# Transposes of attention output and second norm through DMA, other query blocks and merged logits in an adaLN attention and FFN layer

## The chip, the cores and the metric

The program runs on one core of a Trainium2 chip. The metric is the device time of one execution in microseconds. Three runs of the kernel before gave 216.83, 216.92 and 216.99 us, median 216.92 us.

## What is computed

One transformer layer on 2048 tokens of width D = 448 in bf16. The vector `c` gives six modulation vectors; a layer norm, scaled and shifted by two of them, feeds an attention with 16 heads of 28; each query sees 8 keys, at its own position and 2, 4, ... 14 before it. Its output goes through `wo`, is gated and added to `x`. A second modulated norm feeds a gated silu FFN of width 1792.

```python
mod = (silu(c) @ w_mod).reshape(1, 6, 1, -1)          # sa, ca, ga, sb, cb, gb
h = layernorm(x) * (1 + ca) + sa
q, k, v = split_heads(h @ wqkv)                       # 16 heads of 28
idx = pos[:, None] - arange(8)[None, :] * 2           # masked where < 0
attn = softmax(einsum('bhsd,bhswd->bhsw', q, k[idx]) * 28 ** -0.5)
x = x + ga * (einsum('bhsw,bhswd->bhsd', attn, v[idx]) @ wo)
h = layernorm(x) * (1 + cb) + sb
x = x + gb * (silu(h @ w1) @ w2)
```

## The kernel before

The keys of a token have its parity, so the tokens are split by parity (`par`) into two sequences of 1024. A token tile is 128 tokens of one parity; a chunk `k` is 256 tokens of each parity, four tiles, and there are four chunks. Within a parity the 1024 queries are cut into nine blocks `b` (`BQ = 114`, the last of 112), each with 128 keys that begin 14 tokens of the original sequence before it; `HALO` columns of zeros in `qk` stand for keys before the first token.

For each chunk, `norm1` (the class `Norm`, lines 404 to 450) takes statistics on DVE (`stat`, L412 and L413), the inverse deviation on POOL (`rstd`, L416 and L417), normalises on DVE (`norm`, L421), transposes a tile on PE (`tr`, L427 for three pieces of 128 columns, L429 twice for the last 64, which is kept on both halves of the partitions) and scales and shifts on ACT or DVE out of PSUM (`mod`, L436 or L438) into `h1`. `project` multiplies by `wqkv`: q and k into `qk` (matmuls L516, casts L520), v for each block (L539, casts L529).

For each block and parity, `logits` computes 16 heads in two calls of eight small matmuls (L569; contraction over the 28 rows of a head, keys on the partitions of the result), with an Exp on ACT behind each call (L577), and `mask` multiplies by a band of ones on DVE (L599). `values` multiplies by v (L626), normalises on DVE (L631, L633) into a tile `o`, transposes it on PE (`tr`, L639 and L641) into `ps_ot` and copies that on ACT or DVE (`tc_`, L644) into `oT`. `out_proj` (L663) contracts over the 448 rows of `oT` and adds the result to `x_all` on DVE (L666).

`ffn1` is a second `Norm` with L427 to L438 into `h2`, and seven pairs of 128x512 tiles of `ps_h` (L687 for three full pieces of the contraction, L689 for the last 64 rows) with a Silu behind each (L693). `ffn2` (L711) sums 14 matmuls of 448 columns for each token tile, adds on DVE (L716) and stores through SP (L717).

A contraction over 448 is three pieces of 128 rows and a rest of 64. For the rest, two independent matmuls use the two halves of the array:

```python
for kk in range(KT):                                  # L538, and in the same way L661
    for par in range(2):
        w = wqkv[:, kk, 2 * D:3 * D] if kk < 3 else wqkv3[half(par), 1, :]
        T.matmul(ps[:, par, 0:D], lhsT=h[rows_of(kk, par), kk, par, b0:b0 + 128], rhs=w, ...)
```

All of it is recorded as operations of a `Plan` with engine, estimated time, dependencies and buffers; `emit` then issues them in the order of the table of numbers `ORDER` (L43), in which a letter picks ACT or DVE where either can do it. Every engine executes its own instructions strictly in that order. PSUM has three tiles of two banks (`big`) and two of one (`one`). The attention blocks and FFN chunks alternate as in `SEQ` (L40): blocks 0 to 4, chunk 0, blocks 5 and 6, chunk 1, blocks 7 and 8, chunks 2 and 3, because Exp and Silu need different tables on ACT. At the start, matmuls on a tile `junk` (L349) keep PE at work. The loads stand first on SP's queue. At the end a count of finite normalisers decides on a second, safe computation, which does not run here.

## Time and profile before

| | before |
|---|---|
| median of three runs | 216.92 us |
| the profiled execution, its own time | 217.79 us |
| its span in the trace | 216.1 us |
| PE busy, matmuls | 201.6 us (93%), 1652 matmuls |
| DVE, ACT, POOL busy | 111.8, 107.3, 21.6 us |
| mean granted TensorE clock | 0.987 of full speed |
| packets of the main DMA queue, share of 16 engines | 15.5% |

Busy times of one engine do not overlap, those of different engines do. The trace names a group by its source line and by what it writes and reads (`ps_h<-h,w`), with the buffer numbers left out. PE is pipelined, so the time that one matmul takes from the stream is the distance between starts, and not its duration; the chain of waits gives that distance for each run of matmuls.

### The profile page before, as it was taken

Reading aid. Unit: us, or ns where it says so; the run is one execution under the profiler, and the core shown is the slowest. Engines: PE = TensorE matmul, PEld = TensorE weight load, DVE = VectorE, ACT = ScalarE, POOL = GpSimd, SP = SyncE. Lnnn points to the kernel's source line nnn. Section 1 sums busy time; section 2 is a strip of 40 time slices with the busy share of each in tenths; the row PEclk is TensorE's granted clock in tenths of the full one; section 3 lists DMA queues with packets and bytes.
Section 4 is the critical chain, followed back from the end, with each engine's and each line's share of the span. In section 5 each row is a group of like instructions: output and inputs, shape, how many; then the busy total and the mean of one; then the engine's idle time right before and its main releaser. Section 6 shows DMA issues by size and latency. Waiting matters only on the chain.

```text
span 216.1 us, 3926 instructions
## 1 busy us (share of the span) xinstructions
PE 201.6 (93%) x1652; PEld 96.3 (45%) x1652; DVE 111.8 (52%) x246; ACT 107.3 (50%) x127; POOL 21.6 (10%) x65
## 2 busy tenths in 40 slices
PE   5799999859999999999999999999998999999990
PEld 1273364434455555434534444555543443445540
DVE  3608934798679886255361620898518441102220
ACT  2006538784487487744755966860453243550000
POOL 6501530000000330010100000111000110000000
PEclk9999999988999999999999999999999999999998
DMA  6999920000000000000000000000100000001111
GB/s 220 321 397 324 353 90 3 0 0 3 0 3 2 3 0 3 0 0 0 3 2 21 24 0 3 0 24 21 42 3 21 0 18 6 21 2 44 46 46 29
DMA packets 7936, 11.33 MB, mean 52 GB/s; under 512 B 552, under 2 KB 6696, under 8 KB 7912
## 3 DMA queue, kind: packets, MB, share of 16 engines
q1 hardware_dynamic: 7904, 11.01, 15.5%
q8 instruction: 15, 0.25, 0.5%
q14 instruction: 9, 0.07, 0.1%
q10 hardware_dynamic: 8, 0.00, 0.0%
HBM read 9.18 MB, written 1.84 MB: 51 GB/s over the span
## 4 chain that ended last, share of the span: by engine, by line
PE 88%; DVE 4%; ACT 2%; DMA 2%; issue 1%; ACTq 0%
PE ps_y L711 20%; PE ps_h L687 18%; PE ps_qk L516 13%; PE ps_v L539 6%; PE ps_wo L663 5%; PE ps_t L427 4%; PE ps_o L626 4%; PE ps_h L689 4%; PE ps_l L569 3%; PE ps_w L349 3%; PE ps_m L378 3%; PE ps_t L429 3%; DMA c<-in_c_dram 2%; PE ps_ot L639 1%; PE ps_ot L641 1%; DVE w L739 1%
## 5 line engine op out<-in xcount | busy, mean ns | idle before, releaser
L711 PE MATMUL ps_y<-w,both 128*128 128x448 bf16 x224 | 45.8, 353 | 0.0
L687 PE MATMUL ps_h<-h,w 128*128 128x512 bf16 x168 | 40.8, 380 | 0.0
L693 ACT ACTIVATE both<-ps_h 128x1024 bf16<-128x1024 f32 x28 | 28.6, 1024 | 23.5 <-PE ps_h L689 14.3
L577 ACT ACTIVATE p<-ps_l 128x912 bf16<-128x912 f32 (+1 forms) x36 | 31.3, 933 | 8.7 <-PE ps_l L569 8.5
L711 PEld LDWEIGHTS <-both 128*128 128x128 bf16 x224 | 20.5, 98 | 19.8 <-issue 1.2
L516 PE MATMUL ps_qk<-h,wp 128*128 128x512 bf16 (+1 forms) x128 | 28.5, 392 | 0.0
L716 DVE TENSOR_TENSOR ot<-ps_y,x_all 128x448 bf16<-128x448 f32 x16 | 9.9, 622 | 32.2 <-PE ps_y L711 32.2
L687 PEld LDWEIGHTS <-w 128*128 128x128 bf16 x168 | 14.7, 97 | 18.9 <-issue 4.0
L520 ACT CAST qk<-ps_qk 128x1024 bf16<-128x1024 f32 x14 | 14.1, 1013 | 16.5 <-PE ps_qk L516 16.5
L416 POOL TENSOR_TENSOR rs<-mv,epsb 128x2 f32<-128x2 f32 (+1 forms) x18 | 6.1, 337 | 151.2 <-DVE mv L413 151.2
L412 DVE BATCH_NORM_STATS2 st<-x_all 128x6 f32<-128x448 bf16 x32 | 19.5, 609 | 2.6 <-DMA x_all<-in_A_x_dram 2.4
L599 DVE TENSOR_TENSOR p<-p,maskb 128x1824 bf16<-128x1824 bf16 (+1 forms) x18 | 19.5, 1094 | 2.4 <-ACT p L577 2.3
L436 ACT ACTIVATE h<-ps_t,modc 128x512 bf16<-128x512 bf16 x14 | 10.1, 774 | 20.7 <-DVE h L438 18.4
L438 DVE TENSOR_SCALAR h<-ps_t,modc 128x512 bf16<-128x512 bf16 x18 | 8.9, 539 | 13.9 <-ACT h L436 8.3
L516 PEld LDWEIGHTS <-wp 128*128 128x128 bf16 (+1 forms) x128 | 9.3, 98 | 15.0 <-issue 7.0
L666 DVE TENSOR_TENSOR x_all<-ps_wo,x_all 128x448 bf16<-128x448 f32 x16 | 9.5, 615 | 9.7 <-PE ps_wo L663 9.7
L539 PE MATMUL ps_v<-wqkv,h 128*128 128x448 bf16 (+1 forms) x72 | 14.3, 355 | 0.0
L569 PE MATMUL ps_l<-qk 28*128 28x114 bf16 (+1 forms) x288 | 11.7, 210 | 2.3 <-ACT p L577 1.2
L421 DVE TENSOR_SCALAR xn<-x_all,mv,rs 128x448 bf16<-128x448 bf16 x32 | 11.6, 385 | 3.9 <-POOL rs L417 3.9
L663 PE MATMUL ps_wo<-wo,oT 128*128 128x448 bf16 (+1 forms) x64 | 12.8, 354 | 0.3 <-ACT p L577 0.3
L417 POOL TENSOR_TENSOR rs<-rs,negh 128x2 f32<-128x2 f32 (+1 forms) x18 | 12.1, 670 | 1.4
L631 DVE RECIPROCAL rc<-ps_o 114x16 f32<-114x16 f32 (+1 forms) x18 | 4.5, 252 | 14.4 <-PE ps_o L626 14.2
(78 smaller groups left out, 185.2 us busy)
## 6 DMA issues: line engine op xcount, KB each, us to landing
x_all<-in_A_x_dram SPq DMA_DIRECT2D x4, 448.0 KB, 7.6
out_dram<-ot SPq DMA_DIRECT2D x16, 112.0 KB, 1.7
w<-in_B_w_dram SPq DMA_DIRECT2D x1, 1568.0 KB
both<-in_w_mod_dram SPq DMA_DIRECT2D x1, 1344.0 KB
w<-in_B_w_dram SPq DMA_DIRECT2D x1, 1344.0 KB, 14.0
wqkv<-in_A_wqkv_dram SPq DMA_DIRECT2D x1, 1008.0 KB, 7.9
both<-in_w_mod_dram SPq DMA_DIRECT2D x1, 672.0 KB, 5.4
wo<-in_A_wo_dram SPq DMA_DIRECT2D x1, 336.0 KB, 10.1
```

The source lines that it names most:

```text
L412: V.bn_stats(out=st[:], in_=x_all[:, us[j], :])
L417: G.tensor_tensor(out=rs[:, j:j + n], in0=rs[:, j:j + n], in1=negh[:, 0:n], op=ALU.pow)
L516: T.matmul(ps[:, j, :], lhsT=w.rearrange("p h d -> p (h d)"), rhs=h[rows_of(kk, j), kk, :, 128:128 + CP], start=start, stop=stop)
L520: return [(either(act_ns(1024), dve_ns(1024)), lambda o, ps: copy_on(o)(out=qk[:, :, g, :, s0:s0 + CP], in_=ps[:].rearrange("p j (t s) -> ...
L539: T.matmul(ps[:, par, 0:D], lhsT=h[rows_of(kk, par), kk, par, b0:b0 + 128], rhs=w, start=(kk == 0), stop=(kk == KT - 1))
L569: T.matmul(ps[:, j, g * nq:(g + 1) * nq], lhsT=key, rhs=q, start=True, stop=True)
L577: S.activation(out=out_, in_=ps[:, :, 0:4 * nq].rearrange("p j (g q) -> p j g q", q=nq), func=ACTF.Exp, scale=SCALE)
L599: V.tensor_tensor(out=p, in0=p, in1=maskb[:, 1 if b == 0 else 0, 0:nq].unsqueeze(1).to_broadcast([128, H, nq]), op=ALU.mult)
L663: T.matmul(ps[:, par, 0:D], lhsT=oT[rows_of(kk, par), kk, par, s0:s0 + 128], rhs=wo[rows_of(kk, par), kk, :], start=(kk == 0), stop=(kk == ...
L687: T.matmul(ps[:, j, :], lhsT=w1[:, kk, c0:c0 + 128], rhs=h[:, kk, :], start=start, stop=stop)
L693: return [(("act", act_ns(1024)), lambda o, ps: S.activation(out=hid[:, k % 2, :, i, :], in_=ps[:], func=ACTF.Silu), after + f2_read.get(k ...
L711: T.matmul(box["ps"][:, 0:D], lhsT=hid[:, k % 2, f % 2, f // 2, 128 * j:128 * j + 128], rhs=w2[:, f // 2 + 7 * (f % 2), :], start=(f == 0) ...
```

## The change

The transposes of the attention output `o` and of the second norm leave PE and become DMA transposes on SP's queue (L669, L465), from SBUF straight into `oT` and `h2`; the second norm is scaled and shifted afterwards, in place in `h2` (L472, L474). The first norm stays on PE, with four transposes of full width in place of five. Block 0 has 128 queries and the other eight have 112, so keys begin at `112 * b` and no halo is needed. A block's two logits calls become one with 16 matmuls whose head rows take turns over the four row groups (L601). Rests of a contraction are either filled up to 128 rows with zeros (the modulation vectors L382, the gates L398) or put so that two rests are neighbours (v and `wo`: even ones end with the rest, odd ones begin with it). For odd positions `o` is written 64 columns further right, and `wo` is held twice, the second time shifted by 64 rows; both are gated. The load of the first `x` chunk is split in two and 392 KB more of `wo` are loaded. `junk` matmuls at the start: 11, then three behind each of the four transposed tiles. Buffers: `v` 8 (9), `xn` two of four tiles each (six single ones), `o` two per parity (three). `Plan` gets SP as an engine; `ORDER` is new.

```diff
+def q_of(b):
+    return 0 if b == 0 else 16 + 112 * b
 def nq_of(b):
-    return min(BQ, SP_ - BQ * b)
+    return 128 if b == 0 else 112
...
-    ld_o = [load(336, wo[:, 0:3, :], rows3(A_wo)), load(56, wo[half(0), 3, :], A_wo[384:D, :]), load(56, wo[half(1), 3, :], A_wo[384:D, :])]
+    ld_o = [load(336, wo[:, 0, 0:3, :], rows3(A_wo)), load(56, wo[half(0), 0, 3, :], A_wo[384:D, :]),
+            load(336, wo[:, 1, 1:4, :], A_wo[K3:D, :].rearrange("(k p) n -> p k n", p=128)), load(56, wo[half(1), 1, 0, :], A_wo[0:K3, :])]
...
             for j in range(KT):
-                    for h in range(1 + (j == 3)):
-                        out_ = ps[0][rows_of(j, h), i, j:j + 1]
-                        c0 = v * D + 128 * j
-                        for k in range(KT):
-                            T.matmul(out_, lhsT=wmod[rows_of(k), k, c0:c0 + (K3 if j == 3 else 128)], rhs=scT[rows_of(k), k:k + 1], ...)
+                    c0 = v * D + 128 * j
+                    for k in range(KT):
+                        T.matmul(ps[0][:, i, j:j + 1], lhsT=wmod[:, k, c0:c0 + 128], rhs=scT[:, k:k + 1], ...)
...
-                for k in range(3):
-                    T.transpose(box["ps"][:, k, 128 * j:128 * j + 128], box[j][:, 128 * k:128 * k + 128], ident[:])
-                for h in range(2):
-                    T.transpose(box["ps"][half(h), 3, 128 * j:128 * j + 128], box[j][:, 384:D], ident[:])
+                for k in range(KT):
+                    T.transpose(box["ps"][:, k, at], box["x"][:, j, 128 * k:128 * k + 128], ident[:])
+                if junk_n:
+                    warm_up(junk_n)
...
+        def on_dma(self, h, waits):
+            def tr(o, j):
+                nc.sync.dma_start_transpose(out=h[:, j:j + 2, :, :].rearrange("p j k t -> p (j k) t"), in_=self.box["x"][:, j:j + 2, :].rearrange("p j n -> p (j n)"))
+            def mod(o, k):
+                for to, from_ in ([(half(1), half(0)), (half(0), half(0))] if k == 3 else [(slice(0, 128),) * 2]):
+                    out_, in_ = h[to, :, k, :], h[from_, :, k, :]
...
             def vmm(o, b=b, held=held):
-                b0 = 128 + BQ * b - 14 - CP * k
-                for kk in range(KT):
+                b0 = 128 + 112 * b - CP * k
+                ks = (0, 1, 2, 3) if b % 2 == 0 else (3, 0, 1, 2)
+                for kk in ks:
...
-        for t in range(2):
-            def mm(o, t=t, held=held):
-                ps = held[0] = bigt("ps_l")
-                for g in range(4):
-                    for j in range(2):
+        def mm(o):
+            for t in range(2):
+                held[t] = bigt("ps_l")
+            for g in range(4):
+                for t in range(2):
+                    for j in range(2):
...
         def tr(o):
-            box["t"] = one.tile([128, KT, 128], BF16, name="ps_ot", tag="one")
-            for kk in range(3):
-                T.transpose(box["t"][:, kk, 0:nq], box["o"][0:nq, 128 * kk:128 * kk + 128], ident[0:nq, 0:nq])
-            for h in range(2):
-                T.transpose(box["t"][half(h), 3, 0:nq], box["o"][0:nq, 384:D], ident[0:nq, 0:nq])
-        def tc_(o):
-            copy_on(o)(out=oT[:, :, par, BQ * b:BQ * b + nq], in_=box["t"][:, :, 0:nq])
+            nc.sync.dma_start_transpose(out=oT[:, :, par, q_of(b):q_of(b) + nq], in_=box["o"][0:nq, :])
...
-            for kk in range(KT):
+            qs = (0, 1, 2, 3) if i == 0 else (3, 0, 1, 2)
+            for q in qs:
                 for par in range(2):
-                    T.matmul(ps[:, par, 0:D], lhsT=oT[rows_of(kk, par), kk, par, s0:s0 + 128], rhs=wo[rows_of(kk, par), kk, :], ...)
+                    kk = q if par == 0 else (q + 1) % KT
+                    rows = slice(0, 128) if q < 3 else half(par)
+                    T.matmul(ps[:, par, 0:D], lhsT=oT[rows, kk, par, s0:s0 + 128], rhs=wo[rows, par, kk, :], ...)
```

What the new order does is seen at three places. The first is SP's queue behind the loads (`o`, `xn`: sources; `ot`: output tiles). Before:

```order
L301 DMA w_79<-in_B_w_dram 128x3x1792
L301 DMA w_80<-in_B_w_dram 64x896 x2
L301 DMA w_81<-in_B_w_dram 128x14x448
L717 DMA out_dram<-ot_111 128x448
L717 DMA out_dram<-ot_112 128x448
```

Now, from the second transposes of the first chunk on:

```order
L465 DMA_TRANSPOSE h_0_87<-xn_81 128x8x128
L669 DMA_TRANSPOSE oT<-o_0_102 128x4x112
L669 DMA_TRANSPOSE oT<-o_0_104 128x4x112
L465 DMA_TRANSPOSE h_1_88<-xn_82 128x8x128 x2
L717 DMA out_dram<-ot_106 128x448
L717 DMA out_dram<-ot_107 128x448
L669 DMA_TRANSPOSE oT<-o_1_103 128x4x112
L717 DMA out_dram<-ot_108 128x448
L669 DMA_TRANSPOSE oT<-o_1_105 128x4x112
```

Where only stores stood behind the loads, 18 transposes of `o` and 8 of `xn` (two token tiles each) stand among the 16 stores; one that comes behind a store waits until the store's tile is there.

The second place is DVE at the second norm of chunk 0, just before the first `ps_h`. Before:

```order
L421 TENSOR_SCALAR xn_83<-x_all,mv,rs 128x448
L421 TENSOR_SCALAR xn_85<-x_all,mv,rs 128x448
L631 RECIPROCAL rc<-ps_o 114x16
L633 TENSOR_TENSOR o_110<-ps_o,rc 114x448
L438 TENSOR_SCALAR h_0_92<-ps_t,modc 128x512 x2
L644 COPY oT<-ps_ot 128x4x114
L599 TENSOR_TENSOR p_107<-p_107,maskb 128x1824
```

Now:

```order
L426 TENSOR_SCALAR xn_81<-x_all,mv,rs 128x448
L664 RECIPROCAL rc<-ps_o 112x16
L665 TENSOR_TENSOR o_0_102<-ps_o,rc 112x448
L633 TENSOR_TENSOR p_101<-p_101,maskb 128x1792
L474 TENSOR_SCALAR h_0_87<-h_0_87,modc 128x4x128 x2
L693 TENSOR_TENSOR x_all<-ps_wo,x_all 128x448 x2
L551 CAST qk<-ps_qk 128x2x2x256
```

The last `xn` tile (first row) now goes to SP's queue; the scaling of `h` follows three instructions later, and the copies into `oT` are gone. Casts of q and k (last row), which for chunk 3 stood behind the first `ps_h`, stand ahead of or around it.

The third place is ACT in the first FFN chunk, around the last Silu before the Exps of block 5. Before:

```order
L693 ACT_TABLE_LOAD
L693 ACTIVATE both<-ps_h 128x2x512 x2
L529 CAST v_95<-ps_v 128x16x28
L693 ACTIVATE both<-ps_h 128x2x512 x5
L577 ACT_TABLE_LOAD
L577 ACTIVATE p_104<-ps_l 128x912 x2
```

Now:

```order
L721 ACT_TABLE_LOAD
L721 ACTIVATE both<-ps_h 128x2x512 x3
L560 CAST v_90<-ps_v 128x16x28
L721 ACTIVATE both<-ps_h 128x2x512 x3
L472 ACTIVATE h_1_88<-h_1_88,modc 128x4x128
L721 ACTIVATE both<-ps_h 128x2x512
L609 ACT_TABLE_LOAD
L609 ACTIVATE p_97<-ps_l 128x896 x2
```

A part of chunk 1's second norm, which needs its transpose, stands ahead of the seventh Silu and of the Exps of block 5.

## Rows read from the trace of the kernel before

**Rows 1.** The page: its head, and busy time by engine.
```profile
span 216.1 us, 3926 instructions
PE 201.6 (93%) x1652; PEld 96.3 (45%) x1652; DVE 111.8 (52%) x246; ACT 107.3 (50%) x127; POOL 21.6 (10%) x65
```

**Rows 2.** Windows: stretch, its length, busy us of PE, PEld, DVE, ACT, POOL, clock, DMA.
```profile
20.06:86.28 66.22, 62.40 (x670) 31.78 (x669) 50.11 (x106) 44.17 (x58) 8.76 (x16) 0.97 0.14 47
86.28:210.44 124.16, 123.35 (x905) 56.67 (x901) 52.02 (x108) 58.97 (x64) 6.16 (x12) 1.00 0.05 15
```

**Rows 3.** Chain of waits, the start: start us, us, engine, tile, line.
```profile
7.17 3.53 PE ps_w L349 x8
10.70 3.15 PE ps_m L378 x40
...
16.57 3.49 PE ps_w L349 x9
```

**Rows 4.** Chain of waits, operations on PE that the change touches.
```profile
28.21 2.81 PE ps_m L378 x40
...
76.45 0.27 PE ps_t L427 x3
...
76.90 0.27 PE ps_t L427 x3
...
110.30 3.35 PE ps_qk L516 x16
...
113.64 0.39 PE ps_o L626 x16
...
136.28 0.26 PE ps_ot L639 x3
...
136.71 0.30 PE ps_l L569 x8
...
138.99 0.33 PE ps_l L569 x16
```

**Rows 5.** Chain of waits, from the last output projection to the end.
```profile
169.32 1.43 PE ps_wo L663 x8
...
176.78 0.27 PE ps_t L427 x3
...
188.09 2.59 PE ps_h L687 x12
...
192.62 17.80 PE ps_y L711 x94
210.44 0.62 DVE ot L716
```

**Rows 6.** Timeline of DVE and of ACT, first scaling of the first norm.
```profile
16.62 1.00 DVE L438 TENSOR_SCALAR h<-ps_t,modc 128x512 bf16<-128x512 bf16 x2 [2.31 <-PE ps_t L429]
17.71 1.45 ACT L436 ACTIVATE h<-ps_t,modc 128x512 bf16<-128x512 bf16 x2 [10.34 <-DVE h L438]
```

**Rows 7.** Groups by line and shape, DVE: busy us, mean ns.
```profile
L599 DVE TENSOR_TENSOR p<-p,maskb 128x1824 bf16<-128x1824 bf16 x16 | 17.4, 1096 | 2.4 <-ACT p L577 2.3
L412 DVE BATCH_NORM_STATS2 st<-x_all 128x6 f32<-128x448 bf16 x32 | 19.5, 609 | 2.6 <-DMA x_all<-in_A_x_dram 2.4
L644 DVE COPY oT<-ps_ot 128x456 bf16<-128x456 bf16 x9 | 3.5, 389 | 2.8 <-PE ps_ot L641 2.8
L520 DVE CAST qk<-ps_qk 128x1024 bf16<-128x1024 f32 x2 | 2.5, 1225 | 1.8 <-PE ps_qk L516 1.8
L738 DVE TENSOR_TENSOR wo<-wo,gbc 128x1792 bf16<-128x1792 bf16 x1 | 1.1, 1082 | 0.0
L633 DVE TENSOR_TENSOR o<-ps_o,rc 114x448 bf16<-114x448 f32 x16 | 10.0, 624 | 0.6
```

**Rows 8.** DMA: time from issue to landing of the stores (L717), and of the `x` loads.
```profile
DMA to landing us min/median/max: 1.7/1.7/2.5
...
x_all<-in_A_x_dram SPq DMA_DIRECT2D x4, 448.0 KB, 7.6
```

More of the change, by code (lines that the diff above doesn't have):

```diff
@@ L259, in rows3 @@
         return ap[0:384, :].rearrange("(k p) n -> p k n", p=128)
-    S.preload_act_table(ACTF.Silu)
-    V.memset(junk[:], 0.0)
-    V.memset(c4[:], 0.0)
+    V.memset(junk, 0.0)
+    V.memset(wmod[half(0), 3, :], 0.0)
     G.memset(ident[:], 0.0)
@@ L281, in layer @@
     P = Plan()
[L282 removed]
+    for r, n in (("big", 3), ("one", 2), ("v", NV), ("p", NP), ("xn", NX), ("o0", 2), ("o1", 2), ("out", len(outb))):
         P.resource(r, n)
@@ L344, in layer, with warm_up @@
     warm = []
-    def warm_up(o):
+    def warm_up(n):
         if not warm:
             warm.append(bigt("ps_w"))
-        T.matmul(warm[0][:, 0, :], lhsT=junk[:, 0:128], rhs=junk[:], start=True, stop=True)
-    w_first = w_last = P.op(("pe", WARM_AT), warm_up if not safe else none, take=("big",), mac=213.0)
-    for i in range(WARM):
-        w_last = P.op(("pe", 213.0), warm_up if not safe else none, [w_last], mac=213.0)
-    P.op(("none", 0.0), none, [w_last], give=((w_first, "big"),))
+        for _ in range(n):
+            T.matmul(warm[0][:, 0, :], lhsT=junk[:, 0:128], rhs=junk, start=True, stop=True)
+    w_first = P.op(("pe", 600.0), none, take=("big",))
+    w_last = P.op(("pe", 213.0 * WARM), lambda o: warm_up(WARM), [w_first], mac=213.0 * WARM)
     sc_op = P.op(("act", 200.0), lambda o: S.activation(out=sc4[:], in_=c4[:], func=ACTF.Silu), ld_c, table="s")
@@ L382, in ev @@
             V.tensor_scalar(out=modc[:, dst0 + 1, :], in0=ps[0][:, 1, :], scalar1=1.0, scalar2=None, op0=ALU.add)
-        a = P.op(("pe", 1050.0), mm, [sct] + loads, take=("one",))
-        return P.op(("dve", 130.0), ev, [a], give=((a, "one"),))
+        a = P.op(("pe", 900.0), mm, [sct] + loads, take=("one",))
+        return P.op(("dve", 150.0), ev, [a], give=((a, "one"),))
     wmod_read = []
@@ L393, in mm @@
             for k in range(KT):
-                T.matmul(ps[0][:, 0:D], lhsT=screp[rows_of(k), k, :], rhs=wmod[rows_of(k), k, v * D:(v + 1) * D], start=(k == 0), stop=(k == KT - 1))
-        a = P.op(("pe", 870.0), mm, [rep] + loads, take=("one",), mac=653.0)
+                T.matmul(ps[0][:, 0:D], lhsT=screp[:, k, :], rhs=wmod[:, k, v * D:(v + 1) * D], start=(k == 0), stop=(k == KT - 1))
+        a = P.op(("pe", 760.0), mm, [rep] + loads, take=("one",), mac=653.0)
         wmod_read.append(a)
@@ L500, in norm1 @@
         after = [x for kk in (k - 2,) if kk >= 0 for x in qk_mm[kk] + v_mm[kk] + [halo[kk + 1]]]
-        n = Norm([4 * k + 2 * i + par for par in range(2) for i in range(2)], {u: ld_x[k] for u in range(4 * k, 4 * k + 4)},
-                 lambda kt: h[:, kt, :, 128:128 + CP], lambda ps: ps.rearrange("p (t s) -> p t s", t=2), 0, after=after, waits=[mod1], behind=h1_tr.get(k - 1, []), n=2 if k else 1)
+        n = Norm([4 * k + j for j in range(4)], {4 * k + j: ld_x[k][j // 2] for j in range(4)}, after=after + h1_tr.get(k - 1, []), n=2 if k else 1)
+        n.on_pe((0, 2, 1, 3), lambda rows, kt: h[rows, kt, :, 128:128 + CP], lambda ps: ps.rearrange("p (t s) -> p t s", t=2), [mod1], 0 if k else JUNK)
+        if k == 0:
+            P.op(("none", 0.0), none, n.trs, give=((w_first, "big"),))
         h1_tr[k] = n.trs
@@ L649, in values @@
             P.need(v_op[bb], [nr])
-        tt = P.op(("pe", 290.0), tr, [nr], take=("one",), give=((a, "o"),), mac=190.0)
-        trs[b, par] = P.op(either(430.0, 305.0), tc_, [tt], give=((tt, "one"),))
+        trs[b, par] = P.op(("sp", 1250.0), tr, [nr] + ld_2, give=((a, f"o{par}"),))
     def out_proj(k, i):
@@ L680, in ffn1 @@
         h = h2[k % 2]
-        nrm = Norm(us_of(k), x1_done, lambda kt: h[:, kt, :], lambda ps: ps, 1, after=f1_read.get(k - 2, []), waits=[mod2])
+        nrm = Norm(us_of(k), x1_done, after=f1_read.get(k - 2, []))
+        nrm.on_dma(h, [mod2])
         def mm(i):
@@ L726, in ffn2 @@
             ad = P.op(("dve", 540.0), add, [prev], take=("out",), give=((first, "one"),))
-            P.op(("none", 0.0), none, [P.op(("none", 2200.0), none, [ad])], give=((ad, "out"),))
+            P.op(("none", 0.0), none, [P.op(("none", 2200.0), none, [P.op(("sp", 550.0), store, [ad])])], give=((ad, "out"),))
     for k in range(NC):
```

234 lines of the change are left out of this document (122 added, 112 removed), and 37 rows, old and new, of the table ORDER.

## Prediction, made before the changed kernel ran

> **What bounds the kernel now.** I read first the busy times of the page: PE has 201.6 of 216.1 us [rows 1], twice what DVE or ACT have. Then the windows, cut where the chain of waits shows the first value matmul (20.06), the first `ps_h` of the FFN (86.28) and the last matmul (210.44). In the first stage, attention with all of chunk 0's second norm, PE is busy 62.4 of 66.2 us, and DVE 50.1; in the second 123.35 of 124.16 us, and DVE and ACT less than half [rows 2]. So PE is the path nearly throughout, and what leaves PE's stream shortens the second stage one to one. In the first DVE is close behind. Ahead of 20.06 PE only fills time: 8 junk matmuls, 40 small ones for the modulation, four transposed tiles, 9 junk [rows 3].
>
> **Prices on PE, from distances between starts in the chain of waits.** A transposed token tile takes 0.45 us (76.45 to 76.90), a transposed block of `o` 0.43 (136.28 to 136.71) [rows 4]. A logits call of eight takes 0.30, but two of them in a row 0.33 for sixteen [rows 4]: the first eight carry most of the cost, and the merged call should have the price 0.33. A tile of the first norm with four full transposes: `ps_y` moves 448 columns in 17.80 / 94 = 0.189 us [rows 5], so 128 take 0.054 and four 0.22, an estimate; it saves 0.23. The 40 small matmuls take 2.81 us [rows 4]; 32 of one shape at the pace of the sixteen logits (0.33 / 16 = 0.021) are 0.7 to 0.9, saving 1.9. The q and k of a chunk are two runs of 3.35, 6.6 in all with the second a little shorter [rows 4]. An output projection is 1.43 [rows 5].
>
> **First stage.** In the new order it takes over chunk 3's q and k (+6.6) and one output projection (+1.4), and loses 12 tiles at 0.23 (2.8), chunk 0's four second-norm tiles (1.8), nine blocks of `o` (3.9), 20 calls that become 10 (20 x 0.30 - 10 x 0.33 = 2.7), and 1.9 of small matmuls. 62.4 + 8.0 - 13.1 = 57.3 us of PE; the neighbouring rests I price at 0.3. DVE gets there, by counting its rows in the order: three more statistics (0.61 and a little more, 2.1), a second gating of `wo` (1.1), four more scalings of `h1` (0.5 each, [rows 6]: 2.0), two more casts of q and k (2.4), five copies fewer (1.9), 0.4 of small things: 50.1 + 6.1 = 56.2 [rows 2, 7]. So PE and DVE both need 57 us: neither can be the slack of the other, and the stage can't end before that.
>
> **The new wait.** Nothing in this trace transposes by DMA. Call L the time from its issue to its landing. Below, a store of 112 KB lands in 1.7 us (at most 2.5); above, the 448 KB `x` loads in 7.6 [rows 8]. The 128 KB of an `o` block are nearest to the store; with something for the two-tile `h2` transposes of 256 KB I take **2.5**. What covers L, from the order: at the first `h2`, DVE does a normalisation (0.62 and the reciprocal, 0.9 in all) and a mask (1.1) behind the last `xn`, PE then the block's values (0.4, [rows 4]), 2.4 in all, while behind the landing ACT still has three scalings of 0.73 ([rows 6, 7]: 2.2) to do; so L is covered by 0.2 alone, and PE stops for 2.3. At the first output projection PE has a logits call, one block's values, four tiles and a value block (0.33 + 0.4 + 0.9 + 1.43 = 3.1) behind the values that it needs, less 1.2 for normalising and the hand-offs: 1.9 covered, 0.6 waited. The other seven output projections have at least 4.4 by the same count and wait for nothing. At chunk 1's second norm, where a part of it stands ahead of the last Silu and the Exps on ACT, 2.9 is covered; at chunk 2's about 2.5. At chunk 3's: PE has 34 `ps_y` matmuls (6.4) and two `ps_h` tiles (2 x 1.6, at 2.59 for 12 matmuls) = 9.6; from the last projection to the transposes went 176.78 - 170.75 = 6.0 [rows 5], and the scalings take 1.3: 2.3 covered, 0.2 waited. SP itself is no bound: 42 issues in some 150 us. But a transposition behind a store waits for that store's sum on DVE; I allow 1 us for it.
>
> First stage: 57 + 2.3 + 0.6 = **60.0** instead of 66.2, -6.2.
>
> **Second stage.** 123.35, less q and k (6.6), one projection (1.4), 12 tiles (5.4), nine `o` blocks (3.9), 16 calls that become 8 (4.2 in the chain, two or three of them adjacent already, to 2.6: 1.6) = 104.4. The 0.8 that PE waits today, the 0.2 above, 1 for SP and 0.9 for rests and an odd order: 107.3 instead of 124.2, **-16.9**. DVE and ACT lose the copies here and keep under 60 us of work.
>
> **Start.** From 7.17 PE has 12 junk matmuls (12 x 0.44 = 5.3 by 3.53 for 8), 16 transposes (2.3, from the 2.72 us between 13.85 and 16.57 for 20) and 32 small matmuls (2.5, at 3.15 for 40) [rows 3]: the last transpose ends near 16 as against 16.57 if PE is as slow as it is there today, at 13 if it speeds up earlier. The scalings follow (today DVE's two, then ACT's two, 2.6 us in a row [rows 6]), but the nine junk matmuls that PE puts behind them (to 20.06) are gone, and values begin with the pieces that DVE does first. I take 17.3, **-2.8**, between 0 and -5. The memsets stand beside the loads of the first `x`, and the 392 KB more of loads behind what the first stage needs first; if they delay it after all, the start gains nothing, which is the bound of 0. The end behind the last matmul, 216.1 - 210.44 = 5.7 us, is the same.
>
> Sum: -2.8 - 6.2 - 16.9 = -25.9, a span of 190.2 and an own time of 217.79 - 25.9 = 191.9. The profiled run before is 0.9 above its median, so the median should be **191.0 us**.
>
> **A rule that speaks against it.** The rows above give a tile on PE 0.45 us, and that stream is the path. The Trainium skill, VectorE: DVE Perf Modes, The three transpose paths, puts a 128x128 transpose at 390 ns on TensorE and 1309 ns through the DMA crossbar, and advises TensorE where PSUM will do; if its figure held for each of the 18 x 4 + 8 x 8 = 136 squares in turn, an estimate from that page is 178 us of transposes and a slower kernel. The same skill, Advanced Engine Details and Errata, X-Bar Transpose (TRN2), says that they run as fast as ordinary DMAs, by which L would be that of a store and the sum 190. No run here shows either yet.
>
> **Rivals.**
> *The first stage stays as long (200).* PE and DVE need 57 us each there and are tied together by PSUM tiles, masks and normalisations; before, DVE had 16 us to spare. If they get in each other's way as much as the shorter work gives, the stage stays at 66.2 and the start gains nothing: 191 + 6.2 + 2.8 = 200.0. For it: both sums are equal. Against: PE waits little even where DVE is busiest.
> *Transposes land one square after another, and it is slower (227).* If each 128-column square costs what a store does, 1.7 us, then L is 6.8 for an `o` block and more for `h2`. With 6.8 everywhere the stalls are 6.6 + 4.9 + 3.9 + 4.3 + 4.5 = 24 at the five places above and 7 x 2.4 = 17 at the seven projections; 41 less the 3 that are in the sum already and 2 of the allowances: 191 + 36 = 227. The point from which it decides is L near 6, where about 31 us of stalls eat the 26. For it: nothing in the trace bounds L but an `x` load of 7.6. Against: that load is four times as large and shared the engines with other loads. The page with 1309 ns is on this side.
> *The merged logits don't overlap (196).* 18 calls at 0.60 instead of 0.33 are 4.9 more. Against: two separate calls already do overlap.
> *The change does nothing by the clock* (within 0.2%, which is about what a measurement here can tell from no change): it would need losses that happen to equal 26 us.
>
> **How the numbers follow.** Forecast 0.65, with its own range 186 to 195; first stage as before 0.18; logits 0.06; all waits hidden and an early start, 184 to 186, 0.03; slower 0.07; no change 0.01. Faster 0.92, same 0.01, slower 0.07. The range takes the start at -5, both waits at L = 1.7 and the second stage at 105 for its low end, 184, and the rival of the first stage with L at 4 (1.5 more at each of two or three places) for its high end, 204; left out is the slow transpose and a little on either side.
>
> **What would show it.** Right: PE loses its time in `ps_t`, `ps_ot`, `ps_l` and `ps_m` and in no other group; `ps_t` has 64 matmuls left, `ps_ot` none; a logits run of 16 in 0.33; DMA transposes that land in 2 to 3 us; the first `ps_h` near 77, the last matmul near 184; DVE busy over 90% between 17 and 77. Wrong: PE waiting for `oT` or `h2` by DMA in many places (L too small); a first stage over 63 us with DVE busy throughout (DVE is the bound) or with both idle (order); a first value matmul still at 20; or a second stage that does not fall by 15, which would say that PE was not the path there.

## The result, and the profile after

| | before | changed |
|---|---|---|
| median, executions | 216.88 us, 4 | 194.58 us, 4 (192.22 to 197.40) |
| ratio, 95% interval | | 0.8888, 0.8844 to 0.8931 |
| the same measured again (first experiment) | 216.55 us, 11 | 194.94 us, 6 (191.84 to 197.86); 0.8931, 0.887 to 0.8993 |
| profiled execution: own time, span, granted clock | 217.79, 216.1, 0.987 | 195.85, 194.1, 0.962 |

The change is 11% faster. Forecast were 191.0 us and 184 to 204; the time lies 3.6 us above the forecast. The ten executions of the changed kernel scatter over 6 us; the lower the mean clock granted to TensorE, the longer, roughly (191.84 us at 1.0, 192.22 at 0.995, 194.30 at 0.982, 197.86 at 0.965, but also 193.19 at 0.976). The ratios leave out the executions that took over 1.5% longer than the fastest of their kernel, the medians are of all.

The page of the changed kernel:

```profile
span 194.1 us, 3585 instructions
PE 176.9 (91%) x1450; PEld 80.2 (41%) x1450; DVE 116.5 (60%) x252; ACT 100.0 (52%) x116; POOL 20.6 (11%) x62
```

PE has 24.7 us less work than in [rows 1], DVE 4.7 more. The windows, cut as in [rows 2] (first value matmul, first `ps_h`, last matmul), with the clock behind POOL's column:

```profile
0.00:12.75 12.75, 9.35 (x72) 4.36 (x73) 8.22 (x30) 1.75 (x3) 6.29 (x34) 1.00 0.85 251
12.75:84.43 71.68, 63.52 (x624) 28.70 (x625) 57.62 (x119) 45.06 (x58) 8.82 (x16) 0.90 0.41 112
84.43:189.30 104.87, 104.05 (x760) 47.15 (x756) 50.04 (x104) 53.21 (x56) 5.45 (x12) 1.00 0.17 43
```

| stretch | before | forecast | this profile | at full clock |
|---|---|---|---|---|
| start | 20.06 | 17.3 | 12.75 | 13.0 to 13.2 |
| first stage | 66.2 | 60.0 | 71.7 | 67 to 68 |
| second stage | 124.2 | 107.3 | 104.9 | 104.9 to 105.3 |
| end | 5.7 | 5.7 | 4.8 | 4.3 to 4.5 |

(The last column is from three profiles with a clock of 0.99 or 1.0, described below: the whole `x` load, the gate left out, the idle work.) So the sum came out nearly right by errors that cancel: the start is 4.5 us shorter than forecast and the second stage 2.4, the first stage 7 to 12 us longer.

PE from the beginning of the changed kernel (timeline: start, us, tile; in brackets what it waited for):

```profile
1.26 4.44 PE L357 MATMUL ps_w<-both 128*128 128x512 bf16 x11 [1.26 <-DVE both L265]
...
9.74 0.81 PE L357 MATMUL ps_w<-both 128*128 128x512 bf16 x3
10.39 0.39 PE L443 MATMUL ps_t<-ident,xn 128*128 128x128 bf16 x4
...
12.75 1.00 PE L571 MATMUL ps_v<-wqkv,h 128*128 128x448 bf16 x4 [1.33 <-DVE h L454]
15.45 3.80 PE L571 MATMUL ps_v<-wqkv,h 128*128 128x448 bf16 x12 [1.69 <-DVE h L454]
```

11 junk matmuls take 4.44 us, 0.40 each; three at 9.74 take 0.65 up to the start of what follows, 0.22 each. PE goes at twice the pace (from 6.5 us on, as the timeline shows), where the kernel before still needed 3.49 us for nine at 16.57 [rows 3]. PE's order is another matter. In the kernel before, the first normalised tile was there at 6.65 us and all four by 9.71, but 8 junk and 40 small matmuls stood ahead of the first transpose, which came at 13.78, and nine more junk behind the last (timelines before, then the changed kernel):

```profile
6.29 0.36 DVE L421 TENSOR_SCALAR xn<-x_all,mv,rs 128x448 bf16<-128x448 bf16 x1
...
13.78 0.50 PE L427 MATMUL ps_t<-ident,xn 128*128 128x128 bf16 x3
```

```profile
6.45 0.40 PE L443 MATMUL ps_t<-ident,xn 128*128 128x128 bf16 x4 [0.65 <-DVE xn L426]
```

Now two of the four tiles' transposes stand ahead of the small matmuls, and the first comes when its tile is there. What then holds the first value matmul in this execution is on DVE:

```profile
11.85 0.39 DVE L482 COPY wp<-wqkv 128x896 bf16<-128x896 bf16 x1 [1.93 <-DMA wqkv<-in_A_wqkv_dram]
12.16 0.99 DVE L454 TENSOR_SCALAR h<-ps_t,modc 128x512 bf16<-128x512 bf16 x2
14.85 0.54 DVE L454 TENSOR_SCALAR h<-ps_t,modc 128x512 bf16<-128x512 bf16 x1 [1.70 <-ACT h L452]
```

A copy waits for the load of `wqkv`, and the scalings, which need nothing of it, stand behind it; between the second and the third of DVE's, ACT scales two pieces.

The transposes that the forecast was least sure of (issue line, its duration on SP in ns, time to landing; first of `o`, then of `xn`):

```profile
L669 SPq DMA_TRANSPOSE oT<-o x18: 1184/1202/1727, 42.8 to 144.7; - x18
...
DMA to landing us min/median/max: 2.3/2.3/3.8
...
L465 SPq DMA_TRANSPOSE h<-xn x8: 1231/1236/1937, 61.4 to 158.2; - x8
...
DMA to landing us min/median/max: 2.7/2.7/2.8
```

L is 2.3 and 2.7 us; 2.5 was taken between the bounds of [rows 8]. PE's matmuls wait for `oT` for 0.2 us in the whole kernel, its weight loads for 1.0; one more stop, of 0.55 us at the last norm, is for a scaling of `h2` that itself waited for its transpose. And the clock, in windows cut by it (the number ahead of the last two):

```profile
11.40:15.30 3.90, 1.03 (x5) 0.23 (x4) 1.75 (x4) 2.01 (x3) 0.00 (x0) 1.00 1.06 360
15.30:18.70 3.40, 3.25 (x11) 0.90 (x12) 3.26 (x12) 2.28 (x4) 0.00 (x0) 0.51 1.04 365
...
29.40:32.70 3.30, 1.05 (x16) 0.88 (x15) 2.05 (x6) 3.25 (x5) 0.00 (x0) 0.96 0.70 240
32.70:39.80 7.10, 6.53 (x20) 2.12 (x21) 7.05 (x13) 3.28 (x6) 0.00 (x0) 0.54 0.02 5
...
54.00:55.70 1.70, 0.78 (x23) 0.56 (x19) 1.70 (x3) 1.61 (x2) 0.00 (x0) 1.00 0.00 0
55.70:59.40 3.70, 3.53 (x24) 1.50 (x24) 3.60 (x9) 2.22 (x4) 1.12 (x2) 0.58 0.14 31
```

Three times PE has stops in a stretch (it is busy 1.03 of 3.90, 1.05 of 3.30 and 0.78 of 1.70 us; the longest single stops are 1.69, 1.98 and 0.76 us), and behind each the clock is at its lower level, 1.2 in place of 2.4 GHz, for 3.4 to 7.1 us.

### The profile page after: what moved, and what is told of

It reads as the page before. It is cut to its first block, busy times and chain, and to the rows that moved or that the text cites. A ratio compares the mean times of both kernels' runs of the same rounds, so it can differ in the third digit from the quotient of the medians.

```text
span 194.1 us, 3585 instructions
## 1 busy us (share of the span) xinstructions
PE 176.9 (91%) x1450; PEld 80.2 (41%) x1450; DVE 116.5 (60%) x252; ACT 100.0 (52%) x116; POOL 20.6 (11%) x62
## 5 line engine op out<-in xcount | busy, mean ns | idle before, releaser
L609 ACT ACTIVATE p<-ps_l 128x896 bf16<-128x896 f32 (+1 forms) x36 | 31.4, 931 | 5.9 <-PE ps_l L601 4.6
L715 PEld LDWEIGHTS <-w 128*128 128x128 bf16 x168 | 15.4, 97 | 19.3 <-issue 3.0
L571 PE MATMUL ps_v<-wqkv,h 128*128 128x448 bf16 (+1 forms) x72 | 18.5, 430 | 5.3 <-DVE h L454 5.0
L633 DVE TENSOR_TENSOR p<-p,maskb 128x1792 bf16<-128x1792 bf16 (+1 forms) x18 | 19.7, 1100 | 2.5 <-ACT p L609 2.3
L420 POOL TENSOR_TENSOR rs<-mv,epsb 128x2 f32<-128x2 f32 (+1 forms) x18 | 4.8, 266 | 134.4 <-DVE mv L417 134.2
L551 ACT CAST qk<-ps_qk 128x1024 bf16<-128x1024 f32 x11 | 11.1, 1010 | 11.5 <-PE ps_qk L547 11.5
L571 PEld LDWEIGHTS <-h 128*128 128x128 bf16 (+1 forms) x72 | 6.2, 108 | 16.1 <-issue 7.2
L665 DVE TENSOR_TENSOR o<-ps_o,rc 112x448 bf16<-112x448 f32 (+1 forms) x18 | 11.2, 624 | 0.6
L560 ACT CAST v<-ps_v 128x448 bf16<-128x448 f32 x14 | 7.1, 534 | 8.1 <-PE ps_v L571 6.5
L659 PEld LDWEIGHTS <-p 128*128 128x128 bf16 x288 | 8.8, 96 | 4.4 <-issue 1.1
## 6 DMA issues: line engine op xcount, KB each, us to landing
wo<-in_A_wo_dram SPq DMA_DIRECT2D x2, 336.0 KB, 11.9
```

Of the source, the lines that this page charges most:

```text
L609: S.activation(out=out_, in_=ps[:, :, 0:4 * nq].rearrange("p j (g q) -> p j g q", q=nq), func=ACTF.Exp, scale=SCALE)
L633: V.tensor_tensor(out=p, in0=p, in1=maskb[:, 1 if b == 0 else 0, 0:nq].unsqueeze(1).to_broadcast([128, H, nq]), op=ALU.mult)
L665: V.tensor_tensor(out=box["o"][0:nq, off:off + D].rearrange("p (h d) -> p h d", d=DH), in0=ps[0:nq, :, 0:DH], in1=r.unsqueeze(2).to_broadc ...
L715: T.matmul(ps[:, j, :], lhsT=w1[:, kk, c0:c0 + 128], rhs=h[:, :, kk, :], start=start, stop=stop)
```

## The experiments

The question was why the first stage did not shorten, with PE's work there at 57 us as forecast. **A**: PE stops for the first norm's scalings, and the half clock behind the stops lengthens the rest. **A'**: the stops themselves, the chain of hand-offs between DVE and ACT in a norm, are what counts. **B** (a rival of the prediction): PE and DVE are both full and get in each other's way. **C**, formed later: what counts is what stands ahead in DVE's queue at a few places. Each run is an edit of the changed kernel.

### The same again, and idle work in PE's stops

> The changed kernel again, to see how its time goes with the granted clock. Theory A (PE stops in front of the first norms' scalings, and the half clock that follows these stops makes the first stage long): executions differ by the clock alone, near 192 us at a granted clock of 0.99 and 194 to 197 at 0.965; if the profiled execution has a clock over 0.99, its first stage (first value matmul to first ps_h) is about 66 us instead of 71.7 and the second stays at 104.9. Theory B (PE and DVE need the same time there and get in each other's way): the first stage is 70 us or more whatever the clock is.

Measured: 194.94 us (0.8931). The profiled execution had a clock of 0.965, and a first stage of 72.9 us; the fastest took 191.84 us at 1.0. Then, with work in the stops (`fill` is the number of the chunk; the 14 matmuls ahead of one block of values are not shown):

```diff
-                    warm_up(junk_n)
+                    warm_up(junk_n + (8 if j == 3 else 0))
+                for _ in range(4 if j == 3 and fill == 1 else 0):
+                    for k in range(KT):
+                        T.transpose(box["ps"][:, k, at], box["x"][:, j, 128 * k:128 * k + 128], ident[:])
+                if j == 3 and fill == 2:
+                    t = onet("ps_j")
+                    for _ in range(32):
+                        T.matmul(t[:, 0:128], lhsT=ident[:], rhs=ident[:], start=True, stop=True)
...
+                for _ in range(8 if b == 0 else 0):
+                    T.matmul(ps[:, 0, 0:D], lhsT=h[:, 0, 0, b0:b0 + 128], rhs=wqkv[:, 0, 2 * D:3 * D], start=True, stop=True)
```

> The changed kernel with about 6 us of idle work on PE put into the stops that its profile shows before 56 us (8 more junk matmuls behind the first four tiles, 8 value matmuls that are overwritten, four repeats of the last transposed tile of chunk 1, 32 products of the identity behind the transposes of chunk 2, and 14 ahead of one block of values). Nothing that is needed starts earlier by it. Theory A: the granted clock stays at full speed up to the first ps_h, the mean clock is over 0.985 in every execution, and the median falls from 194.6 to 191 to 192 with less scatter. Theory B: the clock and the scatter are as before, the time is the same or up to 2 us longer by the work added.

Measured: 192.66 us (191.84 to 193.77, clock 0.991 to 1.0 in all six; 0.8923, 0.888 to 0.8965). Its first stage:

```profile
12.99:80.48 67.49, 62.54 (x695) 31.98 (x694) 57.06 (x118) 44.52 (x58) 8.83 (x16) 1.00 0.39 114
```

The clock stays up in all six, the median falls by 2.3 us and the scatter shrinks from 6 to 2 us, nearly as A expected. But the ratio to the kernel before, from which the slowest executions are left out, is the same (0.8931 and 0.8923), the fastest executions are equal, 191.84, and at a clock of 1.00 the stage still takes 67.5 us. What differs are the executions of 195.5 us and more at 0.969 or less, five of the changed kernel's ten and none of these six. The clock in the stage goes with its length: 72.9 us at 0.91, 71.7 at 0.90, 70.3 at 0.95 and 67.2 to 67.9 at 1.00 in the profiles of five runs. (The mean clock of a whole execution is a rougher sign: two later runs, edited at the start, have 191.30 us at 0.985 and 191.83 at 0.978.) So the clock goes with most of the distance from 192 to 195 and more; it does not tell why the stage is longer than 60. That the filling is what kept the clock up is likely and not shown, for the next run has no filling and 0.99 to 1.0 in all four executions.

### The gate of w2 left out

```diff
-            w2_gated = [P.op(("dve", 535.0), lambda o, f=f: V.tensor_tensor(out=w2[:, f:f + 2, :], in0=w2[:, f:f + 2, :],
+            w2_gated = [P.op(("dve", 535.0), lambda o, f=f: f or V.tensor_tensor(out=w2[:, f:f + 2, :], in0=w2[:, f:f + 2, :],
```

> Six of the seven products that gate w2 are left out (3.3 us of DVE between 37 and 41 us; the output lacks the gate there); nobody waits for them before the second FFN matrix. Theory B: DVE is the bound of the first stage, which ends up to 3.3 us earlier. Theory A': DVE catches up there anyway, under 0.7 us.

Measured: 192.59 us (191.86 to 193.39; 0.8923, 0.8866 to 0.898), clock 1.0 in the profiled execution:

```profile
13.24:80.40 67.16, 58.05 (x624) 27.52 (x625) 54.34 (x113) 44.85 (x58) 8.84 (x16) 1.00 0.42 120
```

DVE has 2.7 us less to do and the stage is as long as with the idle work. So DVE's sum does not set it, and B falls as far as it says that DVE is full. That two engines with 54 to 58 us of work each lose time to one another in many small hand-offs is not excluded by this. PE's real work in the stage is 58.05 us, and 9 us are stops. This profile has stops of 1.98 and 1.69 us too, and no fall of the clock behind them.

### The first norm's scalings all on DVE

```diff
-    11 50v 70v 72a 74 71v 12 52a
+    11 50v 70v 72v 74 71v 12 52a
...
-    22 101 122 23 123 97 191 192 197 98v 126a 159 160 125v 124v 161
+    22 122 23 123 125v 124v 126v 101 97 191 192 197 98v 159 160 161
```

(Pieces of `ORDER`; 70 to 72 and 124 to 126 are the scalings of chunks 0 and 1, 101 is a gating of `wo`.)

> The changed kernel with the scalings of the first norm of chunks 0 and 1 all on DVE (in the profile DVE, ACT and DVE scale one chunk in turn, each waiting for the other: 12.16 to 15.39 us and 30.08 to 33.04 us), and on DVE ahead of the gating of wo in chunk 1. Work on DVE +2 us, on ACT -3 us. Theory A' (this chain of hand-offs is what PE stops for, and the clock falls behind these stops): the 1.69 us stop falls to 0.9 and the 1.98 us stop to nothing, the first stage is 3 us shorter at full clock, and the median falls by 3 to 5 us with less scatter. Theory B (DVE and PE both full in this stage): the same time or 1 to 2 us longer, since DVE has more to do.

Measured: 194.92 us (193.98 to 194.99; 0.9015, 0.8975 to 0.9055), no gain; the first stage took 69.44 us at a clock of 0.98. The stops in front of the values did shrink (1.69 to 1.00 and 1.98 to 0.36 us), but a longer one came, the first row of PE's waits (what waits, for whom, total, times, longest):

```profile
PE ps_qk L547 <- ACT v L560: 3.4, 1, 3.4
PE ps_v L571 <- DVE h L454: 2.9, 3, 1.5
```

On DVE's timeline stands why:

```profile
36.39 3.83 DVE L770 TENSOR_TENSOR w<-w,gbc 128x896 bf16<-128x896 bf16 x7
40.14 0.25 DVE L664 RECIPROCAL rc<-ps_o 128x16 f32<-128x16 f32 x1
40.43 0.62 DVE L665 TENSOR_TENSOR o<-ps_o,rc 128x448 bf16<-128x448 f32 x1
40.97 0.61 DVE L560 CAST v<-ps_v 128x448 bf16<-128x448 f32 x1
```

The cast that frees PE's PSUM tile stands behind the seven gatings of `w2`. PE came there earlier than in the changed kernel, and waited for DVE's queue. A' alone falls, and C is formed: each of the two edits takes away one of two stops in a row, and only both together could shorten the stage.

### Both: scalings on DVE, gatings later

```diff
-    148 103 136 104 137a 106 105 138 238 107 139a 109 235 108 140
+    148 136 137a 138 238 139a 235 140
...
-    426 427 344 343 433 313 228v 229a
+    426 427 103 106 107 344 343 433 313 228v 104 105 229a
...
-    432 431 346
+    432 431 108 109 346
```

> The order of the run with all first scalings on DVE, and besides the seven products that gate w2 moved in DVE's order from 37 to 41 us to the first FFN chunk, where DVE waits (three behind the normalisations of chunk 1's second norm, two behind a value cast, two behind the next statistics). Nothing is left out. Theory C (what counts is what stands ahead in DVE's queue: first the chain of scalings, then, once that is shorter, the gatings, behind which PE stood 3.36 us in the run before): PE's stops of 1.98 and 3.36 us both go, the first stage falls from 67 to about 65 us at full clock, the span to 188, the median to 189 to 190. Theory B (PE and DVE full): the first stage stays at 67 us or more, since DVE's work there is as in the changed kernel less 1 us.

Measured: **189.57 us** (189.52 to 190.59, clock 0.991 to 1.0; 0.8756, 0.8719 to 0.8794), span of the profiled execution 187.8.

```profile
12.81:78.72 65.91, 57.91 (x625) 27.46 (x626) 55.85 (x116) 41.00 (x54) 8.82 (x16) 1.00 0.42 122
78.72:183.67 104.95, 104.05 (x760) 47.15 (x756) 53.79 (x111) 53.20 (x56) 5.45 (x12) 1.00 0.17 43
```

The direction is C's: with neither edit the stage takes 67.9 us (the whole `x` load below, clock 1.00), with one of them 67.2 or 69.4, with both 65.9. C had about 65. B had 67 or more. So these two places are shown to cost about 2 us, and 8.0 us of stops are left (65.91 less 57.91). The ratio falls from 0.8931 to 0.8756, with intervals apart. The second stage takes the gatings (DVE 50.04 to 53.79 us) at no cost.

### And the scalings of chunk 0 ahead of the copy that waits for wqkv

```diff
-    11 50v 70v 72v 74 71v 12 52a
+    11 70v 72v 74 71v 12 50v 52a
```

> The order of the run before (all first scalings on DVE, gatings later), and besides the first copy of wqkv into wp moved behind the five scalings of chunk 0 in DVE's order. In the profiles that copy waits 1.7 to 2.3 us for its load and the scalings, which need nothing of it, stand behind it. If the load of wqkv is what sets the start only through that copy: scalings from 11.4 us on, the first value matmul at 12 instead of 12.8, the second piece at 14 instead of 14.8, and the median 0.5 to 1 us below 189.57. If PE is not the path at that point (DVE's statistics behind it are): no difference within 0.3 us.

Measured: **189.20 us** (188.63 to 190.79; 0.8765, 0.8714 to 0.8816). In the profile the scalings begin at 10.82, values at 11.87 instead of 12.81, and the first stage is 65.77 us: the place is moved by 0.94 us and nothing of it is lost. The medians differ by 0.4 us only, less than the scatter, and the ratios (0.8756 and 0.8765) do not differ. Both versions beat the changed kernel and the one before.

### The start: junk, and the split load

```diff
-WARM, JUNK = 11, 3
+WARM, JUNK = 6, 3
```

> 6 junk matmuls at the start instead of 11, as the kernel before had. Between the last of them, near 3.9 us, and the first transposes at 6.45 us PE has next to nothing, as it had there before. If it is the unbroken work up to 5.8 us that made PE twice as fast from 6.5 us on (0.217 us for a junk matmul, against 0.39 to 0.44 in the kernel before up to 20 us), the matmuls from 6.5 us on take 0.4 us again and the first value matmul comes 1.5 to 3 us later than 12.75. If the speed came with time alone: no difference.

Measured: 192.49 us (191.83 to 194.18; 0.8896, 0.8842 to 0.895). PE in the profile:

```profile
1.26 2.74 PE L357 MATMUL ps_w<-both 128*128 128x512 bf16 x6 [1.26 <-DVE both L265]
...
6.85 1.49 PE L357 MATMUL ps_w<-both 128*128 128x512 bf16 x3
...
10.93 0.81 PE L357 MATMUL ps_w<-both 128*128 128x512 bf16 x3
```

The pace fell back as expected, 0.43 us for a junk matmul from 6.85 to 9.8 us, but the first value matmul came at 13.71, little later than in unedited runs (12.75 and 13.54): the copy that waits for `wqkv` began at 12.80 here. That the fewer junk matmuls are what kept the pace low is not shown: in the next run all 11 are there, and the pace is the same until 10.3 us. What is shown is that the slow pace, kept for 3 us more, costs the start little: runs whose start was not edited have their first value matmul between 12.1 and 13.7 us.

```diff
-    ld_x = [[load(224, x_all[:, 2 * i:2 * i + 2, :].rearrange("p t d -> p (t d)"), x_view[0, :, i, :]) for i in range(2)]]
+    ld_x = [[xload(0), P.op(("none", 0.0), none, chain[0:1])]]
```

> One part undone: the first x chunk is loaded by one DMA of 448 KB again instead of two of 224 KB. If the split load is what brought the first transposes from 13.8 to 6.5 us, they slip by 1 us or so (the two halves land in 2.7 us each), the first value matmul slips by as much, and the median by at most 1 us. If the weights bound the start anyway, no difference.

Measured: 191.84 us (191.30 to 195.19; 0.8857, 0.8792 to 0.8922). The first transposes slip from 6.45 to 6.87 us and the first value matmul stands at 13.00, among those of the split load. It is not the load of `wqkv` that bounds this start. In this profile PE kept its slow pace until 10.3 us (1.28 us for three junk matmuls at 7.27), the copy began at 11.43 without a wait, and the scalings waited for PE's last transposes (timelines of PE and DVE):

```profile
7.27 1.49 PE L357 MATMUL ps_w<-both 128*128 128x512 bf16 x3
...
11.43 0.38 DVE L482 COPY wp<-wqkv 128x896 bf16<-128x896 bf16 x1
12.40 1.00 DVE L454 TENSOR_SCALAR h<-ps_t,modc 128x512 bf16<-128x512 bf16 x2 [0.59 <-PE ps_t L443]
```

The start has two bounds within 1 to 2 us of each other, the load behind which DVE's copy stands and PE's transposes, and from one execution to the next either can be the later.

### The transposes of o back on PE

```diff
-            nc.sync.dma_start_transpose(out=oT[:, :, par, q_of(b):q_of(b) + nq], in_=box["o"][0:nq, :])
+            pt = box["ps"].rearrange("p h d -> p (h d)").bitcast(BF16)[:, 0:512].rearrange("p (k q) -> p k q", k=KT)
+            for kk in range(KT):
+                T.transpose(pt[:, kk, 0:nq], box["o"][0:nq, 128 * kk:128 * kk + 128], ident[0:nq, 0:nq])
+            (S.copy if par else V.tensor_copy)(out=oT[:, :, par, q_of(b):q_of(b) + nq], in_=pt[:, :, 0:nq])
...
```

(Not shown: the PSUM tile is given back only behind the copy, and a transpose is issued earlier than its place where the next block needs the tile.)

> One part undone: the 18 blocks of the attention output are transposed on PE again (four transposes each, into the PSUM tile of the block's values), and copied into oT by DVE for even positions and ACT for odd ones; the rest as changed. By the prediction's prices 18 x 0.43 = 7.7 us more on PE's path, so about +8 us. If the first stage has room on PE for its nine or ten blocks (8 us of stops there), only the second stage's eight cost time: +3.5. If PE now also stops for the normalisation ahead of each transpose: +10 or more.

Measured: 205.42 us (202.97 to 207.63; 0.9501, 0.9428 to 0.9573), 10.5 us more by the medians and 12 by the ratios. Where PE's stream flows, a block's four transposes need 0.21 us (from 115.52 to the next matmul at 115.73), 3.8 for 18, half of the 0.43 of a block with its five in the kernel before [rows 4]:

```profile
115.52 0.37 PE L682 MATMUL ps_o<-ident,o 112*128 112x112 bf16 x4
115.73 0.92 PE L758 MATMUL ps_y<-w,both 128*128 128x448 bf16 x4
```

By its windows (first value matmul, first `ps_h`, last matmul) both stages are longer, the first by 6.1 us and the second by 5.9 against the whole `x` load's 67.9 and 104.9; PE's busy time is 6.0 us more, a part of it by the clock of 0.98 in the first, and its stops are another 6:

```profile
12.12:86.12 74.00, 61.48 (x660) 30.07 (x661) 59.33 (x124) 48.22 (x64) 8.84 (x16) 0.98 0.30 96
86.12:196.84 110.72, 106.67 (x790) 49.18 (x789) 51.20 (x109) 54.17 (x59) 5.47 (x12) 1.00 0.11 31
```

Among the new waits are these of PE's list:

```profile
PE ps_o L682 <- DVE o L667: 2.5, 3, 1.3
PE ps_o L661 <- DVE oT L683: 1.4, 3, 0.5
```

PE stops for the normalisation ahead of a transpose, and for the copy that frees the PSUM tile behind it. The order and the tile were not tuned for this, so 10.5 to 12 is an upper end. The kernel before, whose order was made for transposes on PE, stood for only 0.8 us in its second stage [rows 2], so the stops belong to this edit and are not shown to be what the DMA takes away; what it takes away for certain is the time of the matmuls. About half of that, by 0.21 against 0.43 where the stream flows, four transposes of full width could have saved on PE too; no run tried that in an order made for it.

### Each DMA transpose twice

```diff
-            nc.sync.dma_start_transpose(out=oT[:, :, par, q_of(b):q_of(b) + nq], in_=box["o"][0:nq, :])
+            for _ in range(2):
+                nc.sync.dma_start_transpose(out=oT[:, :, par, q_of(b):q_of(b) + nq], in_=box["o"][0:nq, :])
```

and in the same way for `h2`.

> Every DMA transpose (of the attention output and of the second norm) is issued twice, the second writing the same data behind the first, so that the time from issue to the last landing goes from 2.3 to 2.7 us to about 5. By the covers that the prediction counted (0.2, 1.9, 2.9, 2.5 and 2.3 us at five places and 4.4 at seven projections) PE would stop for about 17 us more. By the trace of the changed kernel, where PE waits 0.2 us for all transposes together, the covers are larger than counted: under 8 us more. In both cases stores are held up too, by at most 2.4 us, at no cost.

Measured: 234.88 us (233.57 to 235.61; 1.0851, 1.0784 to 1.0918), 40 us more than the changed kernel, and slower than before. Of PE's and DVE's waits:

```profile
DVE h L475 <- DMA h<-xn: 21.8, 4, 6.6
...
PE ps_wo L692 <- DMA oT<-o: 16.5, 6, 4.3
```

Both numbers that were expected are far too small. SP held each second transpose until the first had landed (23.2 us of such waits for `oT`, 11.9 for `h`), and behind them in SP's queue stand the other half of a norm or the other parity's block, which PE needs as well; and the clock fell to 0.92. The run doubles SP's queue along with L, and does not tell the two apart. It does show that the gain of this change hangs on transposes that land, and leave SP's queue to the next, in 2 to 3 us.

### Merged logits in halves, and rests not adjacent

```diff
-            for g in range(4):
-                for t in range(2):
+            for t in range(2):
+                for g in range(4):
```

> One part undone in the order of matmuls: the 16 of a block's logits in two runs of eight, each over two row groups, instead of turns over all four; still in one piece. By the prediction's price (two calls in a row took 0.33 us in the kernel before) no change, within 0.5 us. If only the turns over four row groups give 0.33: 16 take up to 0.60, and the time rises by up to 4.9 us.

Measured: 195.30 us (0.892, 0.8839 to 0.9), no difference to the changed kernel's 0.8931. A block's 16 matmuls take 0.33 us (101.40 to 101.73) instead of 0.30 (100.91 to 101.21).

```diff
-                ks = (0, 1, 2, 3) if b % 2 == 0 else (3, 0, 1, 2)
+                ks = (0, 1, 2, 3)
...
-            qs = (0, 1, 2, 3) if i == 0 else (3, 0, 1, 2)
+            qs = (0, 1, 2, 3)
```

> One part undone: the contraction rest of every value and output projection stands at its end again, so that no two rests are neighbours by that. The prediction priced this part at 0.3 us in the first stage and allowed 0.9 for it in all: 0 to +1 us in the median; lost if the scatter by the clock hides it. In the trace a value or projection run of eight should take 1.43 to 1.54 us from start to start either way.

Measured: 195.02 us (0.8915, 0.8837 to 0.8993), no difference that the median could show; the second stage was 105.27 us, among those of the runs with adjacent rests (104.9 to 105.3). PE's busy time there was 104.40 us against 104.05 to 104.09 in most of them. By the traces either part is worth about half a microsecond; the times can show neither.

## Why the prediction was right, and where it was not

**Second stage, right.** Forecast -16.9, measured -19.3. The work removed was priced rightly: 123.35 us less the listed savings gave 104.4, with the 0.8 us of stops that PE had anyway 105.2, and 104.87 was measured. What was too much were the allowances, 2.1 us for SP, rests, an odd order and a wait. `ps_t` has 64 matmuls left, and `ps_ot`, in the chain of [rows 4], is gone:

```profile
L443 PE MATMUL ps_t<-ident,xn 128*128 128x128 bf16 x64 | 4.8, 219 | 1.6 <-ACT p L609 0.9 <-DVE xn L426 0.6
```

**L, right; its covers, wrong.** The 2.5 us taken from the store's 1.7 lie between the measured 2.3 and 2.7. But of the stops worked out from it, 2.3 at the first `h2` and 0.6 at the first projection are not there; at the last norm, where 0.2 was worked out, PE stood for 0.55. The step that failed, at the first `h2`, counted as cover only "the block's values (0.4)" on PE; on PE's timeline a projection and a run of q and k, 4.8 us, stand there too:

```profile
79.26 1.59 PE L690 MATMUL ps_wo<-wo,oT 128*128 128x448 bf16 x8 [0.47 <-DVE v L560]
80.78 3.41 PE L547 MATMUL ps_qk<-h,wp 128*128 128x512 bf16 x16
84.03 0.55 PE L659 MATMUL ps_o<-v,p 128*128 128x29 bf16 x16
84.43 1.46 PE L715 MATMUL ps_h<-h,w 128*128 128x512 bf16 x6
```

while DVE and ACT waited for the landing until 82.4.

The rule of the Trainium skill, Advanced Engine Details and Errata, X-Bar Transpose (TRN2), that transposes go as fast as ordinary DMAs, agrees nearly: 2.3 us for 128x4x112 where a store of 112 KB takes 1.7. The 1309 ns that the Trainium skill, VectorE: DVE Perf Modes, The three transpose paths, gives a 128x128 square cannot stand for each of several in one DMA: a DMA of eight squares lands in 2.7 us, 0.4 more than one of four. The advice of the Trainium skill, VectorE: DVE Perf Modes, Rules for kernel authors, to use TensorE where PSUM will do, is not borne out here, where PE's stream is the path: the run with `o` on PE was 10.5 to 12 us slower, in an order not made for it, and some 4 us of that are the matmuls.

**First stage, wrong.** "57 + 2.3 + 0.6 = 60.0". The 57 was right for both engines (58.05 on PE, 57.4 to 57.6 on DVE), and the prediction called it a lower bound; but it then added the DMA's stops alone, as if PE had no others. At full clock there are 9 to 10 us of stops, few of them for a transpose (0.2 to 0.9 us for `oT` in the whole kernel). Its own signs had this case: "a first stage over 63 us" "with both idle (order)"; DVE was busy for 80 to 85% of the stage and not over 90. Rival "the first stage stays as long" had nearly the right length (66.2; 67 to 68 measured at full clock) and in part the wrong reason: it is not DVE's sum (leaving out 2.7 us of its work changed nothing). Single places in DVE's queue are shown for about 2 us, by the two versions at 65.9 and 65.8; the rest is open, and may be just the two engines in each other's way. And the clock goes with up to 6 us from one execution to the next, of which the prediction, with 0.97 in [rows 2], took no account. That the sum came within 3.6 us of the median is luck: a first stage 7 to 12 us too short against a start and a second stage 6.9 us too long.

**Start, wrong in size.** "I take 17.3" and "between 0 and -5": it is -7.3. The sum let PE begin at 7.17 and end its last transpose "near 16", at the pace of [rows 3]; it began at 6.45 and ended at 10.6, with 0.22 us for a junk matmul in place of 0.44 and 1.06 us for the 32 small ones in place of 2.5. The faster pace is the smaller part: where the slow one lasted until 9.8 and 10.3 us, the first value matmul still came at 13.7 and 13.0. Neither the 11 junk matmuls nor the split load, undone singly, takes the start beyond the 12.1 to 13.7 us of runs with an unedited start. What the two traces show in its place is PE's order, with two tiles' transposes ahead of the small matmuls and three junk matmuls in place of nine behind the last; that is read from the traces, no run undoes it, and so it stays open how much of the 7.3 us it is. (Two slips do not matter: 2.72 us for 20 transposes are 2.2 for 16 and not 2.3, and the terms of the low end of the range give 185 and not 184.)

**The other rivals.** Squares one after another: L was 2.3, not 6.8. That L decides "near 6" was not tested by itself: the doubled transposes were 18 us slower than the kernel before, but with SP's queue held too. Logits that do not overlap: they take 0.30 us, where 0.33 was the price with overlap.

Of the first stage's stops some 8 us are left even in the best version (65.8 against 57.9 of work), none over 1.1 us; these were not followed up.

## What to carry to other kernels

When work leaves the busiest engine, its sum is a bound and not a forecast: in the stage where another engine is as busy, look in that engine's queue for what stands ahead of the instruction that the first waits for, and move what nobody needs yet (here seven gatings and a copy that waits for a load; with the scalings in one piece they gave about 2 us of the stage and 0.9 us of the start, and 8 us of stops were left). Two stops in a row hide each other, so an edit that removes one of them and gains nothing is not yet refuted. A transposition by DMA takes no time of PE, DVE or ACT, but its cover has to be counted on every queue between producer and consumer, the issuing one included.
